# Moving the value matmuls between two projection chunks, with a new chunk order and alternating eviction engines, in a sliding-window attention kernel

## The chip, the cores and the metric

The kernel runs on one core of a Trainium2 chip. The metric is the device time of one execution in microseconds (us). A profile's span is about 1.7 us shorter than the time of the same run. Short names: PE is TensorE, PEld its weight loads, DVE is VectorE, ACT is ScalarE, POOL is GpSimd, SP is the sync engine, from which most DMAs are issued. An *eviction* is the copy of a result out of PSUM, where the matmuls write.

## The reference

Two layers, each an attention block and an MLP block on x of 2048 x 1024. The change touches only the attention:

```python
qkv = (layernorm(x) @ wqkv)            # 32 heads of 32
idx = pos[:, None] - 2 * arange(8)     # 8 keys per query, dilation 2
logits = einsum("bhsd,bhswd->bhsw", q, k[idx]) * scale   # masked
o = einsum("bhsw,bhswd->bhsd", softmax(logits), v[idx])
x = x + o @ wo
```

The MLP mixes tokens (w1: 2048 x 3584, GELU, w2: 3584 x 2048). All inputs and the output are bf16.

## The kernel before

Tokens are stored by parity (DIL = 2), so the dilated window becomes 8 neighbours. A *unit* u is four heads of one parity (NU = 16 units). Each unit has two *visits*, b = 0 and 1, of 512 tokens. A visit does the scores of (u, b), the values of the visit before, and half of the q and k projections of unit u + 1. One projection *chunk* is one of q or k (`part` 0 or 1), one half `n` of 512 tokens: eight 128x512 matmuls into one PSUM bank, then one eviction to `qT` or `kT`.

```python
def qk_chunk(u, wts, part, n):
    ps = m_tile()                      # 2 PSUM buffers
    ...                                # 8 matmuls 128x512
    dst = (qT, kT)[part][g % 2]
    if part:
        nc.scalar.copy(out=dst[:, lo:lo + 512], in_=ps[:])
    else:
        nc.vector.tensor_copy(out=dst[:, lo:lo + 512], in_=ps[:])

def scores(u, b):                      # 32 matmuls 32x64 tiles, 72 columns
    ...     # lhsT=k[hp, lo:lo + HK], rhs=q[hp, lo:lo + HW]   HW = HK + 8
    ...     # ACT: pc = exp(s);  DVE: Pm = pc * band, two halves

def values(u, b, v, oT):               # 128x32 tiles: P @ v, then column sums
    ...     # ACT: rd = ln(sum), rd = exp(-rd);  DVE: oT = acc * rd
```

The score matmuls read 8 q columns past their own block. So the last ones of b = 0 read q half 1 of their unit, and the last ones of b = 1 read q half 0 of the other parity, which is unit u + 1 when u is even.

```python
chunks = [(0, 0), (1, 0), (0, 1), (1, 1)]       # (part, n)
...
for vis in range(2 * NU):
    u, b = divmod(vis, 2)
    ...                                          # loads of wqk, wo
    in_order(scores, u, b)
    if vis:
        in_order(values, *divmod(vis - 1, 2), v, oT)
    for n in range(2):
        if u + 1 < NU:
            in_order(qk_chunk, u + 1, wts, *chunks[2 * b + n])
        else:
            in_order(out_proj, 0, 2 * b + n, oT, wo, res, xa[li], h2)
in_order(values, NU - 1, 1, v, oT)
for c, i in order[4:]:
    out_proj(c, i, oT, wo, res, xa[li], h2)
```

`out_proj` loads the residual tile `xr` by the SP DMA queue, does 16 matmuls, adds `xr` on VectorE (DVE) while evicting (`xn`), and stores. The order of instructions on one engine, DMA issues included, is settled by a scheduler that starts from the program order; `in_order` pins PE only.

The softmax here doesn't subtract the row's maximum and nothing guards it: scores larger than these inputs give would overflow.

## Time and profile before

| | us |
|---|---|
| time, median (3 runs at first; 1324.29 to 1326.09) | 1325.92 |
| span of the profiled run | 1321.9 |
| one visit, mean of the 29 full visits of layer 1, start of scores to start of scores | 4.620 |
| the same visit without waits (one in four) | 4.40 |
| the end of attention, first out-projection visit to last out-projection matmul, layers 1 and 2 | 63.8 and 63.3 |

The end of attention is worked out from the timeline: layer 1 from 217.44 to 282.07, less 0.86 for four early MLP matmuls that stand inside it.

The page's busy table (busy us, share of the span, instructions):

```profile
PE 1280.5 (97%) x9220; PEld 590.7 (45%) x9376; DVE 388.0 (29%) x646; ACT 372.3 (28%) x622; POOL 11.6 (1%) x19
```

TensorE is the limit, and only about 41 us of the span are not PE. Even of these, some 7 are not idle: 156 matmul records are missing from this trace (9220 against 9376 weight loads), and the 46 waits for "issue" below stand where the first matmul of a projection has no record. On the other hand, a PE that is "busy" may also be waiting inside a merged group. The waits view for PE (what waited, for what, us in total, times, longest):

```profile
PE m L333 <- DVE xn L335: 8.0, 6, 3.0
PE m L240 <- issue: 7.3, 46, 0.2
...
PE s L266 <- DVE qT L246: 3.0, 16, 0.2
```

The first is the out-projection, the last the scores. The timeline of the visits shows that the last is larger than it looks (start, duration, engine, line, operation, what ended the idle time before):

```profile
129.84 0.34 PE L266 MATMUL s<-qT,kT 32*64 32x72 bf16 x32
131.84 1.54 DVE L275 TENSOR_TENSOR Pm<-pc,band 64x1152 bf16<-64x1152 bf16 x2 [1.80 <-ACT pc L270]
133.41 0.69 DVE L312 TENSOR_TENSOR oT<-acc,rd 128x512 bf16<-128x512 f32 x1
134.02 0.68 DVE L246 CAST qT<-m 128x512 bf16<-128x512 f32 x1
134.24 0.32 PE L266 MATMUL s<-qT,kT 32*64 32x72 bf16 x28
134.75 0.23 PE L266 MATMUL s<-qT,kT 32*64 32x72 bf16 x4 [0.19 <-DVE qT L246]
...
139.07 0.48 PE L266 MATMUL s<-qT,kT 32*64 32x72 bf16 x32
...
143.61 0.59 PE L266 MATMUL s<-qT,kT 32*64 32x72 bf16 x32
...
148.30 0.34 PE L266 MATMUL s<-qT,kT 32*64 32x72 bf16 x32
```

Visits start at 129.84, 134.24, 139.07, 143.61 and 148.30, so they take 4.40, 4.83, 4.54 and 4.69 us. Where the 32 score matmuls take 0.34, nothing is waited for. At 134.24 there are 28, then a stop, then four: these four read q columns that DVE evicts from 134.02 to 134.70, after two mask multiplies and the oT multiply. Where the group is not cut (0.48, 0.59) the wait hides inside the busy time.

The end of attention in layer 1 (SPq is the DMA queue of the sync engine, PEld a weight load):

```profile
215.82 2.09 SPq L348 DMA_DIRECT2D w<-in_B_w_dram  x2
217.44 0.59 PE L266 MATMUL s<-qT,kT 32*64 32x72 bf16 x32
218.04 0.97 SPq L327 DMA_DIRECT2D xr<-in_A_x_dram  x2
218.57 3.63 PE L333 MATMUL m<-wo,oT 128*128 128x512 bf16 x15
223.56 0.69 DVE L335 TENSOR_TENSOR xn<-m,xr 128x512 bf16<-128x512 f32 x1 [1.83 <-DMA xr<-in_A_x_dram]
224.31 5.30 PE L333 MATMUL m<-wo,oT 128*128 128x512 bf16 x16 [2.11 <-DVE xn L335]
...
227.02 0.15 PEld L333 LDWEIGHTS <-oT 128*128 128x128 bf16 x1 [0.28 <-issue]
...
227.44 0.15 PEld L333 LDWEIGHTS <-oT 128*128 128x128 bf16 x1 [0.28 <-issue]
```

The residual loads leave the queue at 218.04, behind two w1 loads (weights of the MLP). The second of these, the fifth in all, left at 217.54, when the last projection matmul that read its buffer had ended (217.53); the first xr followed 0.50 us later. It then took 5.40 us to land (223.44). The first `xn` can't run until 223.56, both projection buffers are full by then, and PE waits 2.11 us. Afterwards 16 matmuls take 5.30 instead of 3.6: weight loads come 0.42 us apart, twice the usual 0.216.

### The profile page before, as it was taken

The page shows a single profiled execution, that of the slowest core. Times are in us where ns is not written, and L with a number is a line of the kernel's source. Part 1 is how long each engine was busy: PE and PEld are TensorE (multiplying, and loading weights), DVE is VectorE, ACT ScalarE, POOL GpSimd, SP SyncE. Part 2 cuts the span into 40 slices and gives each one's busy share as a digit, 9 for nine tenths or more (in the row PEclk, how much of TensorE's full clock was granted, in tenths as well). Part 3 has the DMA queues.
Part 4 walks back from the last instruction along what each step waited for, and adds up shares of the span by engine and source line. Part 5 has one row for each costly group of instructions (what it writes and reads, how often), then busy time and mean ns, then how long its engine had stood idle before and what let it go on. Part 6 is the DMA issues. An engine that isn't in the chain of part 4 may idle for free.

```text
span 1321.9 us, 20836 instructions
## 1 busy us (share of the span) xinstructions
PE 1280.5 (97%) x9220; PEld 590.7 (45%) x9376; DVE 388.0 (29%) x646; ACT 372.3 (28%) x622; POOL 11.6 (1%) x19
## 2 busy tenths in 40 slices
PE   6999999999999999999999999989999999999998
PEld 2444444444444444444444444444444444444443
DVE  8136666850000012323210566668200000111111
ACT  4346665541111110000023666654211111000000
POOL 3000000000000000000000000000000000000000
PEclk9999999999999999999999999999999999999999
DMA  9521111462222226456431101134522222334420
GB/s 247 120 65 34 34 34 59 147 180 71 79 81 62 74 70 172 116 140 172 120 89 45 49 7 34 34 104 152 151 80 64 86 68 67 112 103 121 127 90 32
DMA packets 192201, 121.95 MB, mean 92 GB/s; under 512 B 34416, under 2 KB 173680, under 8 KB 192112
## 3 DMA queue, kind: packets, MB, share of 16 engines
q1 hardware_dynamic: 192000, 120.61, 32.7%
q8 instruction: 73, 1.20, 0.4%
q0 software_dynamic: 112, 0.01, 0.1%
q14 instruction: 16, 0.13, 0.0%
HBM read 96.48 MB, written 16.78 MB: 86 GB/s over the span
## 4 chain that ended last, share of the span: by engine, by line
PE 85%; DVE 7%; ACT 4%; DMA 2%; issue 2%; SPq 0%; DVEq 0%; ACTq 0%
PE s L403 15%; PE s L360 15%; PE m L240 10%; PE m L223 8%; PE acc L403 7%; PE m L403 7%; PE m L360 7%; PE acc L360 7%; PE m L333 7%; DVE Pm L275 3%; ACT pc L270 3%; DVE oT L312 1%; DVE qT L246 1%; DMA xr<-xb 1%; DMA xr<-in_A_x_dram 1%
## 5 line engine op out<-in xcount | busy, mean ns | idle before, releaser
L360 PEld LDWEIGHTS <-w 128*128 128x128 bf16 x1792 | 175.3, 98 | 211.4
L403 PEld LDWEIGHTS <-w 128*128 128x128 bf16 x1792 | 175.3, 98 | 211.4
L240 PE MATMUL m<-hT,wqk 128*128 128x512 bf16 x962 | 220.5, 379 | 8.2 <-issue 7.3
L360 PE MATMUL s<-h,w 128*128 128x512 bf16 x880 | 201.7, 379 | 0.9
L403 PE MATMUL s<-g,w 128*128 128x512 bf16 x882 | 198.8, 379 | 0.7
L406 DVE SCALAR_TENSOR_TENSOR xo<-s,b_sb,xs 128x512 bf16<-128x512 f32 x32 | 24.0, 751 | 539.0 <-PE s L403 532.6
L240 PEld LDWEIGHTS <-wqk 128*128 128x128 bf16 x1024 | 95.3, 98 | 119.7 <-issue 12.9
L275 DVE TENSOR_TENSOR Pm<-pc,band 64x1152 bf16<-64x1152 bf16 x128 | 96.4, 753 | 114.1 <-ACT pc L270 112.0
L333 PE MATMUL m<-wo,oT 128*128 128x512 bf16 x500 | 113.6, 383 | 8.7 <-DVE xn L335 8.0
L223 PE MATMUL m<-wv,hT 128*128 128x512 bf16 x502 | 112.2, 383 | 3.8 <-ACT hT L206 3.2
L360 PE MATMUL acc<-h,w 128*128 128x512 bf16 x438 | 103.0, 379 | 0.5
L403 PE MATMUL acc<-g,w 128*128 128x512 bf16 x438 | 100.1, 379 | 0.5
L403 PE MATMUL m<-g,w 128*128 128x512 bf16 x436 | 98.7, 379 | 0.6
L360 PE MATMUL m<-h,w 128*128 128x512 bf16 x438 | 98.1, 379 | 0.4
L170 ACT ACTIVATE ln<-mv,eps 128x1 f32<-128x1 f32 x64 | 18.8, 294 | 253.2 <-DVE mv L178 253.1
L270 ACT ACTIVATE pc<-s,shift 128x576 bf16<-128x576 f32 x128 | 88.0, 741 | 1.2
L333 PEld LDWEIGHTS <-oT 128*128 128x128 bf16 x512 | 49.9, 98 | 70.7 <-issue 13.3
L223 PEld LDWEIGHTS <-hT 128*128 128x128 bf16 x512 | 50.2, 99 | 65.0 <-ACT hT L206 3.7
L367 ACT ACTIVATE g<-s,b_sb 128x1024 bf16<-128x1024 f32 x28 | 31.2, 1114 | 165.2 <-PE s L360 150.2
L246 DVE CAST qT<-m 128x512 bf16<-128x512 f32 x64 | 43.6, 681 | 96.5 <-PE m L240 96.5
L244 ACT CAST kT<-m 128x512 bf16<-128x512 f32 x64 | 37.5, 586 | 105.6 <-PE m L240 105.6
L225 ACT CAST v<-m 128x512 bf16<-128x512 f32 x64 | 37.4, 584 | 64.4 <-PE m L223 62.1
(52 smaller groups left out, 579.9 us busy)
## 6 DMA issues: line engine op xcount, KB each, us to landing
w<-in_B_w_dram SPq DMA_DIRECT2D x56, 512.0 KB, 3.8
w<-in_B_w_dram SPq DMA_DIRECT2D x64, 448.0 KB, 4.5
wqk<-in_A_wqkv_dram SPq DMA_DIRECT2D x16, 512.0 KB, 5.5
xa<-xn SPq DMA_DIRECT2D x32, 256.0 KB, 2.0
xs<-xa SPq DMA_DIRECT2D x32, 256.0 KB, 3.3
x<-in_A_x_dram SPq DMA_DIRECT2D x16, 256.0 KB, 8.5
wv<-in_A_wqkv_dram SPq DMA_DIRECT2D x8, 512.0 KB, 5.9
wo<-in_A_wo_dram SPq DMA_DIRECT2D x8, 512.0 KB, 4.1
```

What stands on the lines that cost most here:

```text
L223: nc.tensor.matmul(ps[:], lhsT=hT[:, kt, cols(c, i)], rhs=wv[n][kt // 4][:, kt % 4, :], start=(kt == 0), stop=(kt == KD - 1))
L225: nc.scalar.copy(out=v[c][i][:, n * 512:(n + 1) * 512], in_=ps[:])
L240: mm = nc.tensor.matmul(ps[:], lhsT=wts[part][:, kt, (g % 2) * P:(g % 2 + 1) * P], rhs=hT[:, kt, lo:lo + 512], start=(kt == 0), stop=(kt = ...
L244: nc.scalar.copy(out=dst[:, lo:lo + 512], in_=ps[:])
L246: nc.vector.tensor_copy(out=dst[:, lo:lo + 512], in_=ps[:])
L270: nc.scalar.activation(out=pc[:, 2 * n:2 * n + 2].rearrange("p h t k -> p h (t k)"), in_=ss[n][:, :, 0:HB * HW], func=ACT.Exp, scale=scale ...
L275: nc.vector.tensor_tensor(out=pm[rp, :, b * HB:(b + 1) * HB, r * HK:r * HK + HW], in0=pc[rp], in1=mk, op=ALU.mult)
L333: mm = nc.tensor.matmul(ps[:], lhsT=oT[g][:, cols(c, i)], rhs=wo[n][g // 4][:, g % 4, :], start=(g == 0), stop=(g == NG - 1))
L360: nc.tensor.matmul(pairs[fl][0][dc], lhsT=wt[c][:, i, fl * P:(fl + 1) * P], rhs=h2[c][i][:, dc * 512:(dc + 1) * 512], start=(k == 0), stop ...
L367: nc.scalar.activation(out=g[fb][:, fl, :].rearrange("p (n d) -> p n d", n=2), in_=t[:], func=ACT.Gelu_apprx_tanh, bias=b1_sb[:, ft:ft + 1])
L403: nc.tensor.matmul(aps[dc], lhsT=w2t[ft // HF][:, ft % HF, c::DIL], rhs=g[ft // GF][:, ft % GF, dc * 512:(dc + 1) * 512], start=(ft == 0), ...
L406: nc.vector.scalar_tensor_tensor(out=xo[:, dc * 512:(dc + 1) * 512], in0=aps[dc], scalar=b2_sb[:, i, c:c + 1], in1=xs[:, dc * 512:(dc + 1) ...
```

## The change

The intent: q columns are computed earlier than the scores that read them, the mid-visit chunk is evicted by ScalarE (ACT) and the last one by DVE, and the values get a chunk of PE time between themselves and the scores.

```diff
@@ qk_chunk
-        if part:
+        if n == 0:
             nc.scalar.copy(out=dst[:, lo:lo + 512], in_=ps[:])
@@ the attention loop
-        chunks = [(0, 0), (1, 0), (0, 1), (1, 1)]
+        chunks = [(0, 0), (0, 1), (1, 0), (1, 1)]
@@
             in_order(scores, u, b)
-            if vis:
-                in_order(values, *divmod(vis - 1, 2), v, oT)
             for n in range(2):
+                if n and vis:
+                    in_order(values, *divmod(vis - 1, 2), v, oT)
```

## The prediction

> **What bounds it now.** TensorE: the page's busy table gives PE 97% of 1321.9 us, ACT 28%, DVE 29%; the chain of waits is 85% PE. Its 5632 matmuls of 128x512 follow each other 0.2158 us apart in the timeline (16 take 3.45), alone about 1215 us. The change touches only the two attention stretches, 79.7 to 282 and 730 to 932 us.
>
> **A visit, from the timeline.** It is 32 score matmuls, the value matmuls and 16 projection matmuls. Start to start it cycles 4.40, 4.83, 4.54, 4.69 us, mean 4.615. The 4.40 visit has no waits: 3.45 projection, 0.10 into the scores, 0.27 scores, 0.58 values. The others lose 0.14 to 0.39 us inside the scores: the last score matmuls read q columns whose eviction on DVE has just ended. That eviction (0.68 us) stands in DVE's queue behind two mask multiplies (1.54) and the oT multiply (0.69). The waits view names only 3.0 us of this (scores waiting for DVE qT); the visit times show 0.79 us per four visits.
>
> **The change there.** Both q chunks of the next unit come in one visit, its k chunks in the next, and the first half of each goes to ACT in mid-visit. Every column that the next scores need is then evicted over 1 us early, so 0.20 us per visit goes. Against it stands one more switch of array shape per visit. The Trainium skill, "TensorEngine Tiling (Array Packing)", Key Properties, says that changing tiling mode drains TensorE; here a switch shows about 0.10 us. Scores alone (a layer's first visit, 3.83) cost 0.38; values alone, between out-projections, 0.68 to 0.70. New visit: 3.45 + 0.38 + 0.69 = about 4.52. Saving 0.09 x 58 visits = 5 us. Evictions cost alike (0.59 on ACT, 0.68 on DVE); neither engine becomes the limit.
>
> **The end of attention.** From the last projection to the last out-projection the timeline takes 64.5 and 64 us; the matmuls need 58.7. Out-projection waits 2.1 to 3.0, then 0.5 to 0.7 and 0.8 to 0.9 us for DVE xn, which waits for the residual load xr. That load stands in the in-order SP queue behind five weight loads, the fifth waiting for the last wqk buffer. After the first wait in layer 1 matmuls run 0.43 us apart for some 3 us, a halved clock (the skill's "TensorE: Matmul & The Clock Gate", Part 1, has the half rate after idling). In the new order the first xr precedes that fifth load, later ones alternate with stores, and a values block between out-projections gives evictions time. My estimate: 0.5 us of waits left and 0.25 of switches, 59.5 us; saving 4 to 5 us per layer, 9 in all.
>
> All of it is on the critical path. **Sum:** 1325.9 - 5 - 9 = about 1312 us, range 1306 to 1320. Faster by over 2% 0.03; within 2% 0.96; slower 0.01.
>
> **In the profile:** visits even at 4.5 us; no scores waiting for DVE qT; PE waiting for DVE xn under 2 us in all (8.0 now); first xr issued about one visit (4 to 5 us) earlier against the out-projection's start; the MLP stretches unchanged (about 193 us each).
>
> **What would make it wrong.** A switch between projection and values of 0.2 us instead of 0.1 cancels the visits' gain; a new wait in the visits, for the single accumulator pair or for a projection PSUM buffer (DVE's late second eviction), at 0.1 us x 58, does too; xr loads that are still late keep part of the 9 us.

## The result, and the profile after

1307.89 us (4 runs, 1307.58 to 1308.40) against 1326.01 (4 runs, 1324.29 to 1327.86). The ratio is 0.9863, with a 95% interval of 0.9846 to 0.9881. Ratios here are the mean time of one kernel's runs over that of the other's of the same rounds, so not quite the ratio of the medians quoted. The gain of 18 us is far outside the noise.

Busy table and waits view of PE in the kernel after:

```profile
PE 1289.1 (99%) x9376; PEld 581.1 (44%) x9376; DVE 388.1 (30%) x646; ACT 384.0 (29%) x622; POOL 11.6 (1%) x19
```

```profile
PE s L205 <- DVE x L184: 9.3, 2, 8.3
PE m L223 <- ACT hT L206: 3.3, 2, 2.5
```

These two waits are the whole list, and both belong to the start of the kernel (they stood there before as well). The waits for qT and xn are gone. The busy shares must not be compared (97% to 99%): this trace has all 9376 matmul records, that of before lacks 156. A visit in the timeline:

```profile
106.19 0.34 PE L266 MATMUL s<-qT,kT 32*64 32x72 bf16 x32
...
106.46 1.90 PE L240 MATMUL m<-hT,wqk 128*128 128x512 bf16 x8
...
108.09 1.54 DVE L275 TENSOR_TENSOR Pm<-pc,band 64x1152 bf16<-64x1152 bf16 x2 [1.01 <-ACT pc L270]
...
108.40 0.59 ACT L244 CAST qT<-m 128x512 bf16<-128x512 f32 x1 [0.34 <-PE m L240]
...
108.89 1.90 PE L240 MATMUL m<-hT,wqk 128*128 128x512 bf16 x8
...
110.73 0.34 PE L266 MATMUL s<-qT,kT 32*64 32x72 bf16 x32
110.93 0.68 DVE L246 CAST qT<-m 128x512 bf16<-128x512 f32 x1
```

All scores take 0.34 now. This visit projects the two q halves of the next unit. The first is evicted on ACT by 108.99, 1.7 us before the next scores; every second time these read it (here they do not, for u is odd). The second is evicted after the next scores have started, and is read only one visit later. In the visits that project k, the first half goes to ACT at the same place, and it is the half that the next scores read. The end of attention:

```profile
210.76 0.54 SPq L327 DMA_DIRECT2D xr<-in_A_x_dram  x1
...
214.71 0.34 PE L266 MATMUL s<-qT,kT 32*64 32x72 bf16 x32
...
214.98 3.63 PE L333 MATMUL m<-wo,oT 128*128 128x512 bf16 x16
...
215.29 0.61 SPq L327 DMA_DIRECT2D xr<-in_A_x_dram  x1
...
218.18 0.69 DVE L335 TENSOR_TENSOR xn<-m,xr 128x512 bf16<-128x512 f32 x1
...
219.14 1.04 PE L333 MATMUL m<-wo,oT 128*128 128x512 bf16 x4
```

The first residual load is issued 3.95 us before the first out-projection visit starts; it was 0.60 us after it. PE never waits for it. (The last line is cut by the window; the group has 16 matmuls in 3.63.)

| us, from the timelines | before | after | saved |
|---|---|---|---|
| first scores to first out-projection visit, layer 1 / layer 2 | 137.79 / 137.73 | 134.94 / 134.94 | 2.85 / 2.79 |
| end of attention, layer 1 / layer 2 | 63.8 / 63.3 | 58.3 / 58.3 | 5.5 / 5.0 |

That is 16 us of saving, as the spans say (1321.9 less 1305.9). The timed runs say 18, because the profiled run of before (1323.66 us) was the fastest of its kernel.

### The profile page after: what moved, and what is told of

Read it like the earlier page. It is cut to its first block, busy times and chain, and to the rows that moved or that the text cites. A ratio compares the mean times of both kernels' runs of the same rounds, so it can differ in the third digit from the quotient of the medians.

```text
span 1305.9 us, 20991 instructions
## 1 busy us (share of the span) xinstructions
PE 1289.1 (99%) x9376; PEld 581.1 (44%) x9376; DVE 388.1 (30%) x646; ACT 384.0 (29%) x622; POOL 11.6 (1%) x19
## 4 chain that ended last, share of the span: by engine, by line
PE 97%; DVE 1%; DMA 1%; ACT 0%; issue 0%; SPq 0%
PE m L240 18%; PE s L403 15%; PE s L360 15%; PE m L223 9%; PE m L403 7%; PE m L360 7%; PE acc L360 7%; PE acc L403 7%; PE m L333 7%; PE acc L294 1%; PE s L266 1%; PE acc L298 1%; DMA x<-in_A_x_dram 1%; DVE bn L176 0%; DVE xn L335 0%; PE acc L290 0%
## 5 line engine op out<-in xcount | busy, mean ns | idle before, releaser
L240 PE MATMUL m<-hT,wqk 128*128 128x512 bf16 x1024 | 241.8, 380 | 0.0
L240 PEld LDWEIGHTS <-wqk 128*128 128x128 bf16 x1024 | 90.6, 98 | 108.6 <-issue 12.9
L312 DVE TENSOR_TENSOR oT<-acc,rd 128x512 bf16<-128x512 f32 x64 | 44.0, 687 | 39.7 <-ACT rd L310 39.7
L246 DVE CAST qT<-m 128x512 bf16<-128x512 f32 x32 | 21.8, 682 | 95.3 <-PE m L240 95.3
```

The lines of the kernel that those rows point to most:

```text
L240: mm = nc.tensor.matmul(ps[:], lhsT=wts[part][:, kt, (g % 2) * P:(g % 2 + 1) * P], rhs=hT[:, kt, lo:lo + 512], start=(kt == 0), stop=(kt = ...
L312: nc.vector.tensor_tensor(out=oT[g][:, lo:lo + hb * P], in0=acc[:, 0, :], in1=rd[:], op=ALU.mult)
```

## The experiments

Theory A: there are two independent gains, (1) scores no longer wait for q evictions, and (2) the residual loads start earlier, less (3) about 0.1 us per visit for one more change of array shape. The rivals are in the expectations. "Visit" is the mean of the 29 full visits of layer 1 in the profile (for e2 28 of them, without its first, which took 4.95 us; with it the mean is 4.537), and "end" the end of attention in layers 1 and 2 as defined above. Before, in the rounds of each group, had medians of 1325.1 to 1325.6.

| kernel | time | ratio | visit | end |
|---|---|---|---|---|
| before | 1325.1 to 1326.0 | 1 | 4.620 | 63.8, 63.3 |
| the change | 1307.89 | 0.9863 | 4.521 | 58.3, 58.3 |
| e1 order and engines, values together | 1310.37 | 0.9891 | 4.414 | 62.6, 61.8 |
| e2 values apart, nothing else | 1309.60 | 0.9881 | 4.522 | 58.6, 58.4 |
| e3 values apart only at the end | 1313.65 | 0.9912 | 4.620 | 58.4, 58.4 |
| e4 order, engines, values apart only at the end | 1301.52 | 0.9820 | 4.414 | 58.3, 58.3 |
| e5 order alone | 1319.24 | 0.9951 | 4.519 | 65.7, 64.8 |
| e6 engines alone | 1324.11 | 0.9989 | 4.606 | 63.7, 67.1 |
| e7 xr on another queue, nothing else | 1314.67 | 0.9914 | 4.620 | 58.7, 58.7 |
| e8 order, engines, xr on another queue | 1302.78 | 0.9827 | 4.414 | 58.6, 58.6 |
| e9 the change, one more block per visit | 1320.21 | 0.9960 | 4.740 | 58.3, 58.3 |

All nine computed the right result. The edits are against before, except for e9.

### e1: order and engines, values straight after scores

```diff
-        if part:
+        if n == 0:
-        chunks = [(0, 0), (1, 0), (0, 1), (1, 1)]
+        chunks = [(0, 0), (0, 1), (1, 0), (1, 1)]
```

> New chunk order and new eviction engines, values still straight after scores. Theory A (the change has two independent gains: score matmuls no longer wait for q columns, and the residual loads at the end of attention start earlier): visits fall from 4.615 to about 4.40 to 4.45 us, cheaper than the 4.52 of the full change because one array switch less; the end of attention keeps its 63 us per layer. Total about 1314 us (12 less than before). Rival B (setting the visits apart is what frees the evictions): scores still wait, visits stay above 4.55, total above 1322 us.

Measured: 1310.37 us, visits 4.414, no scores waiting for qT. Rival B falls. The total is 3 to 4 us better than expected because the end got shorter too, by 1.2 and 1.5 us: PE still waited for `xn` (7.5 us in six waits), but no stretch of halved clock followed in its profiled run.

### e2: values apart, nothing else

```diff
             in_order(scores, u, b)
-            if vis:
-                in_order(values, *divmod(vis - 1, 2), v, oT)
             for n in range(2):
+                if n and vis:
+                    in_order(values, *divmod(vis - 1, 2), v, oT)
```

> Only the values moved between the two chunks; chunk order and engines as before. Theory A: q is now the mid-visit chunk and its DVE eviction is queued ahead of the oT multiply, so the scores do not wait either: visits 4.52, end of attention 58.3 us per layer, total about 1308 us, the same as the full change. Rival C (chunk order and engines carry the visits' gain): visits stay at 4.7, total about 1317 us.

Measured: 1309.60 us, visits 4.522, end 58.6 and 58.4. Rival C falls. Moving the values alone gives, within the intervals, all of the change's gain (0.9866 to 0.9896 against 0.9846 to 0.9881). With the values apart, q is the mid-visit chunk, and the instruction order puts its DVE eviction ahead of the oT multiply: in one visit the mask multiplies end at 105.87, qT is evicted from 105.90 to 106.59 and oT follows at 106.62. The next scores start at 106.84, so the margin is 0.25 us, where the change has 1.7. In the change as a whole the new order and engines add little: either of the two cures is enough for the scores. The traces show what is added: in e2 the first full visit of each layer still waits (4.95 and 4.88 us, 4.51 in the change) and the ends are 0.3 and 0.1 us longer, 1.2 us in all; the spans differ by 1.3 (1307.2 and 1305.9).

### e3: values apart only in the two visits with out-projections

```diff
-            if vis:
+            if vis and u + 1 < NU:
                 in_order(values, *divmod(vis - 1, 2), v, oT)
             for n in range(2):
+                if n and vis and u + 1 == NU:
+                    in_order(values, *divmod(vis - 1, 2), v, oT)
```

> Kernel before, with the values set apart only in the two visits per layer that hold out-projections. Theory A: visits unchanged at 4.615, end of attention 58.3 instead of 63.5 us per layer: about 10 to 12 us less than before, 1314 to 1316 us. If the end's gain came from the chunk order instead, the total stays near 1326.

Measured: 1313.65 us, visits unchanged at 4.620, end 58.4. A move in four of the 64 visits brings two thirds of the gain. The instruction order of the SP queue changes with it: the first xr load now stands before the fourth w1 load (it leaves at 193.93, before at 218.04), the second still behind the fifth, and later xr loads alternate with stores.

### e4: e1 and e3 together

> New order and engines, values apart only in the two out-projection visits of each layer. Theory A: both gains without the extra array switch in the 58 other visits (about 0.11 us each): visits 4.40 to 4.42, end 58.3 us per layer, total about 1302 us, 6 less than the full change. Rival: if values straight after scores bring a wait back, visits at 4.52 or more and no gain over 1308 us.

Measured: 1301.52 us (1301.16 to 1301.91), as expected, with visits of 4.414 and ends of 58.3. This beats both kernels: 6.4 us less than the change. That is the extra 0.107 us (4.521 less 4.414) of 58 visits.

### e5 and e6: order alone, engines alone

```diff
 e5:
-        chunks = [(0, 0), (1, 0), (0, 1), (1, 1)]
+        chunks = [(0, 0), (0, 1), (1, 0), (1, 1)]
 e6:
-        if part:
+        if n == 0:
```

> Kernel before with only the new chunk order (both q chunks, evicted by DVE, in one visit; both k chunks, evicted by ScalarE, in the next). Theory A (what matters is that the columns the next scores need were computed a chunk earlier): most of the waits go, visits 4.41 to 4.47, about 1311 to 1314 us, near the 1310.4 of order and engines together. If the engine of the eviction is what matters, the two q evictions still end behind the oT multiply, visits stay at 4.55 or more and the total above 1320 us.

> Kernel before with only the new eviction engines (chunk order as before: q half 0 and k half 0 both on ScalarE in one visit, q half 1 and k half 1 both on DVE in the next). Theory A: the wait for q half 0 goes (0.14 us per four visits), the waits of the unit's first visit for q half 1 stay (0.26 and 0.39): visits about 4.58, total about 1323 us, 2 to 3 less than before. If the engine is what matters, total near 1311.

Both missed in size. e5 took 1319.24 us and its visits 4.519, so half of the wait stays. Its timeline shows why:

```profile
119.48 0.69 DVE L312 TENSOR_TENSOR oT<-acc,rd 128x512 bf16<-128x512 f32 x1
...
120.08 1.28 DVE L246 CAST qT<-m 128x512 bf16<-128x512 f32 x2
120.34 0.21 PEld L266 LDWEIGHTS <-kT 32*64 32x64 bf16 x29 [0.42 <-issue]
120.34 0.32 PE L266 MATMUL s<-qT,kT 32*64 32x72 bf16 x28
120.82 0.23 PE L266 MATMUL s<-qT,kT 32*64 32x72 bf16 x4 [0.16 <-DVE qT L246]
```

Both q evictions now stand behind the oT multiply on DVE, and one visit in four still reads q half 0 of the next unit as it is evicted. The other three run free. The rest of e5's shortfall is at the end of attention, which was longer in its profiled run than in that of before (65.7 against 63.8): two of its waits for xr were followed by a halved clock. That run was the slowest of its four (1321.96; the others 1317.61 to 1319.37).

e6 gained nothing (interval 0.9969 to 1.0009), and its visits took 4.606. The wait for q half 0 went, as expected, but the wait for q half 1 became 0.43 us in every second visit: visits of 4.40 and 4.83 us alternate, 9.23 per unit, where before had 4.40, 4.83, 4.54 and 4.69, 18.46 for two units. My sum took the waits of before as separate costs. They were not: with one wait gone, the next visit starts earlier and waits longer for the same queue on DVE. With the values straight after the scores, the engines alone give nothing, the order alone half of the visits' gain, and both together all of it (e1).

### e7: residual loads on another DMA queue

```diff
-        nc.sync.dma_start(out=xr[:], in_=res(c, i))
+        nc.gpsimd.dma_start(out=xr[:], in_=res(c, i))
```

> Kernel before with the residual loads xr issued from GpSimd's own DMA queue instead of the SP queue; nothing else moves. Theory A (the end of attention waits because xr stands behind the fifth weight load and the stores): the wait of 2 to 3 us falls below 1 us and the halved clock after it goes; PE waits for DVE xn about 2 us in all instead of 8.0, total about 1318 us. Rival D (two out-projections back to back leave VectorE no time, only a values block between them helps): waits stay near 8 us, total 1325.

Measured: 1314.67 us, 10.7 less than before in its rounds. The waits view and the timeline of the GpSimd queue:

```profile
PE s L266 <- DVE qT L246: 3.0, 16, 0.2
PE m L333 <- DVE xn L335: 0.4, 2, 0.2
```

```profile
200.85 0.56 POOL L327 DMA_DIRECT2D xr<-in_A_x_dram  x1 [188.28 <-DVE oT L312]
210.08 0.55 POOL L327 DMA_DIRECT2D xr<-in_A_x_dram  x1 [8.66 <-DVE oT L312]
```

In this run the first out-projection visit starts at 219.29, so the first load leaves 18.4 us ahead. The waits for `xn` fall from 8.0 to 0.4 us with nothing moved on PE. Rival D falls: VectorE had time enough, and the place in the SP queue was the cause. The Trainium skill says in "DMA: Bandwidth & Descriptors", section "Anatomy of one DMA — SWDGE (gpsimd) path", that a semaphore wait is done by the issuing sequencer before dispatch. The section is about GpSimd's path, while xr in before is issued by SP. If it holds there too, a load that waits for its buffer holds up every load behind it in that queue; the trace of before agrees (fifth w1 load held until 217.54, xr 0.50 us after it), and this pair of runs shows what it cost, 10.7 us. I had expected 2 us of waits to stay.

### e8: order and engines of e1, xr queue of e7

> New order and engines, values straight after scores in every visit, residual loads on GpSimd's DMA queue: both causes removed without setting anything apart. If the two causes are all there is and independent, 1325.4 less 14.7 (order and engines together) less 10.7 (other queue), plus the 2 to 3 us of the end's gain that order and engines already had: 1300 to 1303 us, visits 4.415, PE waiting for DVE xn under 1 us. If setting the values apart at the end does something more than the queue does, it stays above 1304 us.

Measured: 1302.78 us, visits 4.414, ends 58.6, waits for `xn` 0.6 us in all. Both causes are removed without setting anything apart, and the time is within 1.3 us of e4. So the two causes account for the gain; what the values between out-projections add beyond an early load is 0.3 us per layer, net of their own changes of array shape (58.6 against 58.3).

### e9: the change with one more block of small matmuls per visit

```diff
 values():   the P @ v matmuls stay between the two chunks
+            the column-sum matmuls, ln, exp and oT multiply are kept for later
 qk_chunk(): for kt in range(KD):
+                if kt == KD // 2 and mid is not None:
+                    mid()              # in the second chunk: the kept column sums
```

> The full change with one more passage from projection to small matmuls and back in 58 visits: the column-sum half of the values is moved into the middle of the second projection chunk; no matmul is added or removed. Theory A (a passage costs about 0.11 us, from 4.521 against 4.415 us): visits 4.63 us, about 6 us more than the full change, 1314 us. If the 0.11 us were a hidden wait for PSUM or for an eviction, a further split would cost nothing or several tenths: 1308, or above 1320.

Measured: 1320.21 us, 12.3 more than the change, visits 4.740. Not the 0.11 but 0.22 us per visit. By the letter of the expectation, a total above 1320 spoke for the rival, a hidden wait. The waits view lists none but the two at the start, but a wait of 0.1 us could hide from it. The trace decides: the matmuls that start the new blocks (114.38, 115.35 and 115.69 below) are recorded without any semaphore wait. The timeline shows two equal pieces (line numbers are shifted by the edit; L242 is the projection):

```profile
114.03 0.42 PE L297 MATMUL acc<-Pm,v 128*32 128x136 bf16 x16
114.38 1.04 PE L242 MATMUL m<-hT,wqk 128*128 128x512 bf16 x4
115.35 0.40 PE L303 MATMUL acc<-Pm,ones 128*32 128x512 bf16 x4
115.58 0.18 PE L311 MATMUL acc<-Pm,ones 128*32 128x24 bf16 x4
115.69 1.04 PE L242 MATMUL m<-hT,wqk 128*128 128x512 bf16 x4
116.66 0.34 PE L269 MATMUL s<-qT,kT 32*64 32x72 bf16 x32
```

From the v matmuls to the projection 0.35 us pass, where they pass on to the column sums in 0.25 when these follow directly (103.78 to 104.03 in the timeline of the change). From the projection's start to the column sums 0.97 us pass, for four matmuls of 0.216, so 0.11 more than their work. My expectation had counted the block as one switch. It is two, one in and one out. Counting changes of array shape per visit (projection 128x128, scores 32x64, values 128x32): e1 has 3, the change 4, since scores to values was a switch already, and e9 has 6. The visits are 4.414, 4.521 and 4.740: 0.107 us for the fourth, 0.110 us for each of the last two. What inside such a passage takes the time (the new shape itself, or the first weight load of the new block, which comes only after the last matmul of the old one) is not separated here.

## Why the prediction was right, point by point

The time lies in the range (1306 to 1320), about 4 us below the expected 1312. The range alone proves little, for e1, e2, e3, e5 and e7 fall into it too (1309.60 to 1319.24); the terms of the sum are what was tested.

- **What bounds it.** Right. PE is at 99% in the profile after, and nothing but PE stands in the chain of waits to speak of (97%).
- **Visits.** Right in size: 4.52 expected, 4.521 measured, 5.6 us saved against 5. The wait of 0.20 us per visit went whole, and one switch came at 0.107 us. The cause was told too narrowly: the prediction credits order and engines. e1 shows that these do it on their own, but e2 shows that the values' move alone does it as well, by changing the order of DVE's queue. In the change, one cure is redundant but for about 1 us. In e4 and e8 the values' move in the 58 other visits, with its switch, is left out.
- **End of attention.** The mechanism, a late xr behind the fifth weight load, is shown by e7. The saving was put at 9 us and was 10.5: the ends fell to 58.3 us, while I had left 0.5 us of waits per layer that did not appear. The half-sentence that a values block gives evictions time turned out not to matter (e7, e8).
- **The rest of the difference, about 2 us,** is the kernel before, whose profiled run was faster than its median. Its time depends on how late xr lands. The first such wait was 2.11 and 3.03 us in before, 2.01 and 1.71 in e1, 2.42 and 2.88 in e5, 2.14 and 4.02 in e6 (layers 1 and 2 of one profile each). The runs of a kernel with the late load scatter over 2 to 6 us (e6: 1322.06 to 1327.77), those of a kernel without it over 0.3 to 1.5 us. The granted clock goes with it: in the rounds of the experiments it is 0.997 to 0.999 in the runs of before, and 0.999 or 1.0 in every run of a kernel without the late load. That the late landing alone makes this scatter is argued, not shown.
- **What would have made it wrong.** A switch of 0.2 us (it was 0.107), a new wait (none appeared), late loads (none).

## What to carry to other kernels

When PE waits for an eviction, look at what stands ahead of it in the evicting engine's queue, and let the data that the next stage reads be produced one chunk earlier. Waits on one queue are not additive, so taking away half of them may give nothing (e6). A load that waits for its buffer held up the loads behind it in the same DMA queue (before); moving urgent loads to an idle queue is a one-line test, and here it gave more than half of the gain. Setting small matmuls apart between large ones is not free: count the changes of array shape, here 0.11 us each.

## What the Trainium skill lacked or had wrong

- "TensorEngine Tiling (Array Packing)", Key Properties, says that changing the tiling mode drains TensorE and gives no time. Here one change, with the weight load that comes with it, cost 0.107 to 0.110 us at full clock (3, 4 and 6 changes per visit: 4.414, 4.521, 4.740 us).
- "TensorE: Matmul & The Clock Gate", Part 1, gives one idle window of about 3.4 us as what brings back the half rate. Here waits of 2.11 us (before) and 2.28 us (e5) were followed by it, 16 matmuls taking 5.30 us, while waits of 3.03 us (before, layer 2) and 2.42 us (e5) were not, 16 taking 3.61. Its remark that the window is free-running is borne out: in the traces' clock records the changes between full and half rate lie whole multiples of 3.413 us apart (before: 208.21 and 1092.27 us, 61.0 and 320.0 of them; e5: 215.04, 634.88 and 443.73, 63.0, 186.0 and 130.0). With windows laid on these points, those in attention that were followed by half rate held 2.11 us (before), 2.28 and 2.88 (e5) and 3.10 (e6) without a matmul, by the modelled ends; those with 2.03 (before, layer 2) and 2.06 (e5) were not followed by it. So what counted here is the idle time inside one window, and less than a whole window was enough; the 3.03 us wait fell across two.
- None of the pages read for this case says that the modelled ends of matmuls can cover a wait, so that a profile shows it as busy. Here the last four scores of the visit at 143.61 start 0.24 us after the one before them, and the records leave a gap of 0.05. In all, the waits view named 3.0 us for the scores, where the visits of before lost about 12 us (0.20 us in each of 58, on average).
